# Three output projections by seven products of sums: a change to an attention and gated feed-forward kernel on one core

## The chip, the cores and the metric

The kernel runs on one core of a Trainium2 chip. The core has engines with queues of their own: TensorE (PE; its weight loads are listed as PEld), VectorE (DVE), ScalarE (ACT), GpSimd (POOL) and SyncE (SP), which issues nearly all transfers. TensorE multiplies a stationary tile of up to 128x128 with a moving tile of up to 512 columns and adds the result into PSUM; the other engines work on PSUM (not GpSimd) and on SBUF. The metric is the device time of one execution in microseconds, as the median of the runs.

## The reference

```python
scores = scale * q_c @ k_c^T          # 8 batches x 8 heads, in chunks of 64 positions
attn = softmax(scores); out = attn @ v_c
x = out as [4608 tokens, 512]
g = x @ w_gate;  val = x @ w_val      # [512, 1536] each
y = (g * sigmoid(g) * val) @ w_out    # [1536, 512]
```

Everything is float32. The attention is local to chunks of 64 and small; the three large products make the work.

## The kernel before

Float32 products are made from pairs of a rounded upper part and a rest (`split`: ScalarE casts the upper part, VectorE subtracts it from the whole). Each product is the sum of three matmuls: rest x upper, upper x rest, upper x upper.

The 4608 tokens are nine blocks of 512 (`N`); d_ff is twelve steps `f` of 128. Blocks 0 and 1 and block 2 come first. Blocks 3 to 8 are three pairs, loop `for b in range(3, NB, 2)`, L1306. For a pair, `both_steps` (L1193) runs the twelve gated steps for both blocks together. `gated_pair` (L1152) makes gate and value of two blocks by seven products of sums in place of eight products: the x of the pair is held as seven quarter-size sums `pair.x[0..6]`, the weights as `factors` loaded two steps ahead (L1149), and `seventh` (L878) runs six matmuls of 512 columns for each of the seven. The products go into three PSUM banks, and since products 2, 4 and 6 are added onto product 0 in its bank (`ps1`), ScalarE has to copy the bank (to `h`, then `v`) or VectorE to add it before the next product may go there. SiLU and a multiplication give the step's `h` for the first block and `h2` for the second.

The output projection of the first block stands between these products: `turns` (L889) runs `project` (L537) for the step before, 12 matmuls of 512 columns (4 row tiles of 128 tokens, 3 each, L552 to L554) into four PSUM banks `ps_o`. The `h2` of the second block is kept, and `second_steps` (L1211) runs its twelve projections behind the gated steps, 144 matmuls, while VectorE and ScalarE prepare the next pair's x (`later`). Attention for the next pair (scores, softmax, 32x32 transposes on VectorE, columns) stands in the gated steps as well: `bursts`, `middle`, `behind`.

The orders of TensorE, ScalarE and VectorE are those in which the code is written; those of GpSimd and of SyncE's transfers are set by a scheduler that plans a timeline. Transfers issued by SyncE wait in one queue, so one that has to wait holds up those behind it. Tiles come from pools with a fixed number of buffers, and the wait for a free buffer follows from the pool and the tag.

Of the kernel before, what the change touches and what calls it, by code (L numbers as in the profile page):

```python
# [33 lines left out]
def attn_then_gated_ffn(ctx: ExitStack, tc: tile.TileContext, qk, v, wgv, wo, out):  # L34
# [163 lines left out]
    def save_w(f):  # L198
        kept_w[f] = store.tile([P, 2, 4 * Q], F32, name=f"w{f}")
        nc.sync.dma_start(out=kept_w[f], in_=w_both[f].bitcast(F32))  # L200
# [298 lines left out]
    def out_of_two(f, tag):  # L499

        two = const.tile([P, 2, 2, DM], F32R, name="two", tag=tag)
        nc.sync.dma_start(out=two.bitcast(F32), in_=two_o[f // 2])
        return [(two[:, i, 0], two[:, i, 1]) for i in range(2)]

# [30 lines left out]
    before = []  # L535

    def project(parts, wo_f, which=range(T)):  # L537
        (a, f, hh, hl), (woh, wol) = parts, wo_f
        if not hasattr(a, "o"):
            a.o = [ps_o.tile([P, DM], F32, name="ps_o") for _ in range(T)]  # L540
        for t in which:
            ts, o = slice(t * P, (t + 1) * P), a.o[t]
            final = a.b * N + (t + 1) * P == NT
            ends = final and f == a.steps[1]
            left, right = slice(0, DM // 2), slice(DM // 2, DM)
            parts_of = [(o, slice(0, DM), f == a.steps[0])]
            if ends:
                more = ps_a.tile([P, DM // 2], F32, name="ps_a", tag="ps_a")
                parts_of = [(o[:, left], left, False), (more, right, True)]
            for to, m, first in parts_of:  # L550
                skip = ends and not first
                nc.tensor.matmul(to, hl[:, ts], woh[:, m], start=first, stop=False, skip_group_check=skip)  # L552
                nc.tensor.matmul(to, hh[:, ts], wol[:, m], start=False, stop=False, skip_group_check=skip)  # L553
                nc.tensor.matmul(to, hh[:, ts], woh[:, m], start=False, stop=f in (a.steps[1], a.steps[1] - final), skip_group_check=skip)  # L554
            if final and f == a.steps[1] - 1:
                before.append(ld.tile([P, DM // 2], F32, name="before", tag="qk_t"))
                nc.scalar.activation(before[0], o[:, right], AF.Copy, scale=2.0 ** -8)
            if f == a.steps[1]:

                pools = (hp, "o_sb"), (ld, "v_t")  # L560
                r = a.b * N + t * P

                last = a.b == NB - 1
                halves = 2 if last and t in (0, T - 1) else 1
                for i in range(halves):
                    m = slice(i * DM // halves, (i + 1) * DM // halves)
                    pool, tag = (hp, "hl" if t else "h") if i else pools[t % 2]
                    o_sb = pool.tile([P, DM // halves], F32, name="o_sb", tag=tag)
                    if i and final:
                        nc.vector.scalar_tensor_tensor(out=o_sb, in0=more, scalar=2.0 ** -8, in1=before[0], op0=ALU.mult, op1=ALU.add)  # L570
                    elif i or last and t == T - 2:
                        nc.vector.tensor_scalar_mul(o_sb, o[:, m], 2.0 ** -8)
                    else:
                        nc.scalar.activation(o_sb, o[:, m], AF.Copy, scale=2.0 ** -8)
                    (nc.scalar if final and not i else nc.sync).dma_start(out=out[r:r + P, m], in_=o_sb)
# [568 lines left out]
    def load_weights(f):  # L1144
        tags = (7, 8) if f % 2 == 0 else (9, 10)
        loaded[f] = []
        for kept, tag in zip((kept_w, kept_t), tags):
# [4 lines left out]
    def gated_pair(pair, f, h2, inside, middle):  # L1152
# [23 lines left out]
        if not ending:  # L1176
            turn_of(1)
# [179 lines left out]
```

## Time and profile before

| | us |
|---|---|
| median of 3 runs (lowest, highest) | 891.94 (891.91, 892.08) |
| profiled execution, its own time | 893.19 |
| its span, first to last instruction | 891.4 |
| busy in the span: TensorE | 880.9 |
| weight loads | 729.6 |
| VectorE | 547.2 |
| ScalarE | 388.8 |
| GpSimd | 39.7 |
| transfers: 223.25 MB, mean rate | 250 GB/s |

A row of a group reads: line, engine, operation, written tile <- read tiles, shape, count | busy us, mean ns of one | idle time ahead of the group and what ended it. A row of the timeline reads: start, duration, engine, line, operation. Matmul durations overlap, so TensorE's pace is read from the distance of the starts.

### The profile page before, as it was taken

The numbers are of one execution on the slowest core, as the hardware profiler recorded it, in microseconds if no ns is written. First come the engines' busy times: TensorE is split into PE (matmuls) and PEld (weight loads), VectorE is DVE, ScalarE is ACT, GpSimd is POOL, SyncE is SP. The second block draws the span as 40 slices with busy tenths as digits, with TensorE's granted clock in tenths as the row PEclk, the third lists the DMA queues.
The fourth block names the chain that finished last, engine by engine and source line by source line (L and its number), as shares of the span: only waits on it lengthen the run. The fifth ranks groups of instructions, "written<-read, shape, count | busy, mean of one in ns | idle before, by whom it ended". The sixth has DMA issues, their size and how long they took to land.

```text
span 891.4 us, 14743 instructions
## 1 busy us (share of the span) xinstructions
PE 880.9 (99%) x6034; PEld 729.6 (82%) x6034; DVE 547.2 (61%) x831; ACT 388.8 (44%) x594; POOL 39.7 (4%) x32
## 2 busy tenths in 40 slices
PE   7999999999999999999999999999999999999998
PEld 6788888888888888888888888888888888888886
DVE  5888999673888656776753656767655533333332
ACT  5757777543433345225325444244325432223232
POOL 1100000000055110000000000000000000000000
PEclk9999999999999999999999999999999999999999
DMA  9677778889798777657577757575657575556651
GB/s 358 249 269 279 275 276 320 330 296 350 226 387 276 276 264 242 237 219 255 204 250 291 299 206 270 193 253 225 203 212 281 177 269 202 198 196 232 236 189 47
DMA packets 73314, 223.25 MB, mean 250 GB/s; under 512 B 30752, under 2 KB 31264, under 8 KB 59040
## 3 DMA queue, kind: packets, MB, share of 16 engines
q1 hardware_dynamic: 71664, 219.57, 67.7%
q10 hardware_dynamic: 1584, 2.75, 0.9%
q8 instruction: 47, 0.77, 0.3%
q14 instruction: 19, 0.16, 0.0%
HBM read 178.78 MB, written 43.52 MB: 249 GB/s over the span
## 4 chain that ended last, share of the span: by engine, by line
PE 97%; DMA 1%; DVE 1%; ACT 0%; SPq 0%; issue 0%
PE ps_a L883 27%; PE ps_gv L883 20%; PE ps_gv L478 12%; PE ps_o L552 11%; PE ps_o L554 11%; PE ps_o L553 11%; PE ps_a L290 2%; PE ps_a L368 1%; DMA v_t<-in_v 1%; PE ps_a L468 1%; PE pt L454 0%; PE ps_a L454 0%; DVE z L698 0%; SPq L262 0%; ACT v_t L411 0%; DVE xl L642 0%
## 5 line engine op out<-in xcount | busy, mean ns | idle before, releaser
L883 PE MATMUL ps_a<-x,factors 128*128 128x512 f32 x864 | 219.3, 389 | 0.0
L883 PEld LDWEIGHTS ps_a<-x,factors 128*128 128x128 f32 x864 | 162.2, 188 | 33.7
L883 PE MATMUL ps_gv<-x,factors 128*128 128x512 f32 x648 | 164.4, 389 | 0.0
L883 PEld LDWEIGHTS ps_gv<-x,factors 128*128 128x128 f32 x648 | 121.6, 188 | 25.2
L552 PE MATMUL ps_o<-both,hl 128*128 128x512 f32 x336 | 131.9, 392 | 0.0
L554 PE MATMUL ps_o<-both,hh 128*128 128x512 f32 x336 | 130.7, 389 | 0.0
L553 PE MATMUL ps_o<-both,hh 128*128 128x512 f32 x336 | 130.7, 389 | 0.0
L63 DVE TENSOR_TENSOR hl<-h,hh 128x512 fp32r<-128x512 f32 x98 | 68.2, 696 | 65.5 <-ACT hh L62 65.3
L62 ACT CAST hh<-h 128x512 fp32r<-128x512 f32 x98 | 60.6, 618 | 95.4 <-PE ps_o L554 51.3
L478 PE MATMUL ps_gv<-xh,w 128*128 128x512 f32 x320 | 97.9, 391 | 0.2 <-ACT xh L638 0.2
L887 DVE TENSOR_TENSOR h<-h,ps_gv 128x512 f32<-128x512 f32 x44 | 30.2, 686 | 103.9 <-PE ps_gv L883 103.7
L355 DVE STREAM_TRANSPOSE turned<-s_sb 32x256 f32<-32x256 f32 x192 | 83.7, 436 | 2.7
L522 DVE SCALAR_TENSOR_TENSOR h<-v,h 128x512 f32<-128x512 f32 x88 | 60.8, 691 | 37.7 <-ACT h L1188 33.0
L552 PEld LDWEIGHTS ps_o<-both,hl 128*128 128x128 f32 x336 | 63.1, 188 | 13.5
L554 PEld LDWEIGHTS ps_o<-both,hh 128*128 128x128 f32 x336 | 63.1, 188 | 13.1
L553 PEld LDWEIGHTS ps_o<-both,hh 128*128 128x128 f32 x336 | 63.1, 188 | 12.8
L1188 ACT ACTIVATE h<-ps_a 128x512 f32<-128x512 f32 x36 | 21.5, 598 | 112.1 <-PE ps_a L883 112.1
L478 PEld LDWEIGHTS ps_gv<-xh,w 128*128 128x128 f32 x320 | 59.8, 188 | 12.9 <-ACT xh L638 0.5
L478 PE MATMUL ps_gv<-xl,w 128*128 128x512 f32 x160 | 61.3, 392 | 0.0
L887 DVE TENSOR_TENSOR v<-v,ps_a 128x512 f32<-128x512 f32 x44 | 30.2, 687 | 41.1 <-PE ps_a L883 36.4
L1174 ACT ACTIVATE h<-h 128x512 f32<-128x512 f32 x36 | 22.8, 632 | 52.9 <-DVE h L887 52.9
L887 DVE TENSOR_TENSOR v<-v,ps_gv 128x512 f32<-128x512 f32 x44 | 30.2, 686 | 24.5 <-PE ps_gv L883 24.5
(143 smaller groups left out, 1069.9 us busy)
## 6 DMA issues: line engine op xcount, KB each, us to landing
factors<-w SPq DMA_DIRECT2D x36, 1024.0 KB, 4.8
factors<-t SPq DMA_DIRECT2D x36, 1024.0 KB, 6.1
both<-o SPq DMA_DIRECT2D x70, 512.0 KB, 6.3
w<-w SPq DMA_DIRECT2D x16, 1024.0 KB, 8.1
t<-th SPq DMA_DIRECT2D x24, 512.0 KB, 4.2
two<-o SPq DMA_DIRECT2D x12, 1024.0 KB, 5.2
raw<-in_wgv SPq DMA_DIRECT2D x11, 1024.0 KB, 9.0
qk_t<-in_qk SPq DMA_DIRECT2D x10, 1024.0 KB, 8.1
```

Of the source, the lines that this page charges most:

```text
L62: nc.scalar.copy(out=hi, in_=src)
L63: (engine or nc.vector).tensor_tensor(out=lo, in0=src, in1=hi.bitcast(F32), op=ALU.subtract)
L355: nc.vector.transpose(out=self.turned[to:to + 32, p:p + 2, j, :, 32 * (i % 2):32 * (i % 2) + 32], in_=src[32 * i:32 * i + 32, :, o // 2, 3 ...
L478: nc.tensor.matmul(ps, w, x, start=first and (k, i) == which[0], stop=last and (k, i) == which[-1])
L522: nc.vector.scalar_tensor_tensor(out=h, in0=pv, scalar=2.0 ** -8, in1=h, op0=ALU.mult, op1=ALU.mult)
L552: nc.tensor.matmul(to, hl[:, ts], woh[:, m], start=first, stop=False, skip_group_check=skip)
L553: nc.tensor.matmul(to, hh[:, ts], wol[:, m], start=False, stop=False, skip_group_check=skip)
L554: nc.tensor.matmul(to, hh[:, ts], woh[:, m], start=False, stop=f in (a.steps[1], a.steps[1] - final), skip_group_check=skip)
L883: nc.tensor.matmul(ps, w[u][:, k], x[i][v][:, k], start=first and k == 0 and n == 0, stop=k == NK // 2 - 1 and n == 2, skip_group_check=True)
L887: nc.vector.tensor_tensor(out=t, in0=t, in1=ps, op=ALU.add)
L1174: nc.scalar.activation(h, h, AF.Silu, scale=2.0 ** -8)
L1188: nc.scalar.activation(h2, ps1, AF.Silu, scale=2.0 ** -8)
```

## The change

For each pair, the output projection [1024, 1536] x [1536, 512] is now made by seven products of sums in place of eight. The rows are halved by block, d_ff by even and odd steps, the columns of the output into left and right (`HM`, 256). With A11, A12 the first block's h of even and odd steps, A21, A22 the second's, and B the weights likewise, the seven are A11 B11, A12 B21, and five with S1 = A21 + A22, S2 = S1 - A11, S3 = A11 - A21, S4 = A12 - S2 and sums of the four B.

- In the gated steps only the first two products remain: `Left.project`, 12 matmuls of 256 columns for the step before. They stand in one piece between products 5 and 6, no longer parted over the step (one of four row tiles there and three behind product 6 in steps with attention's products).
- `h` and `h2` stay in `rows`; VectorE makes S3 and S1 of them in steps 3, 4, 8, 9 and 10.
- `second_steps` is replaced by `seven_products`: fifteen units of 24 matmuls of 256 columns. Ahead of each, casts and subtractions split the halves of a later unit (three ahead); banks are copied out (`snapshot`, ScalarE) and added at the end (`finish`, VectorE). The next pair's x is prepared here too.
- The sums of the output weights are made once, in the gated steps of the first pair: GpSimd adds upper and rest of a pair of weight tiles and makes four sums (`out_sums`), ScalarE casts them a step later, GpSimd subtracts (`split_sums`), and four transfers keep them in HBM for all pairs.
- The gated weights' quarter that no product reads is neither kept nor loaded (`save_w`, `load_factors`).
- The transposes of attention are dealt singly: one part ahead of `left.lower`, two at the end of a step.

The order changes on TensorE, ScalarE and VectorE. TensorE before, one gated step of the first pair (`ps_o` is the projection; each group of three is one row tile):

```order
L883 MATMUL ps_a<-x,factors 128x512 x6
L883 MATMUL ps_gv<-x,factors 128x512 x6
L552 MATMUL ps_o<-both,hl 128x512
L553 MATMUL ps_o<-both,hh 128x512
L554 MATMUL ps_o<-both,hh 128x512
```

TensorE of the change, the end of one step and the start of the next:

```order
L1199 MATMUL ps_o<-left,hl 128x256
L1199 MATMUL ps_o<-left,hh 128x256 x2
L858 MATMUL ps_a<-x,factors 128x512 x12
L858 MATMUL ps_gv<-x,factors 128x512 x6
L858 MATMUL ps_a<-x,factors 128x512 x6
```

Product 6 of one step and product 0 of the next follow each other (x12), and nothing stands between product 1 (`ps_gv`) and product 2 (`ps_a`), which adds onto product 0.

ScalarE of the change, from the end of a step of the first pair through the next one (`rows<-ps_a` by L1326 is the SiLU of h2, by L1305 the copy of product 0, `sums<-sums` the cast of GpSimd's sums):

```order
L1326 ACTIVATE rows<-ps_a 128x512
L1169 CAST sums<-sums 128x1024
L1305 COPY rows<-ps_a 128x512
L1307 COPY v<-ps_gv 128x512
L1309 COPY v<-ps_a 128x512
L1313 ACTIVATE rows<-rows 128x512
L1182 CAST hh<-rows 128x512
```

The L1169 cast is new and stands ahead of the copy; before, a step was copy, copy, copy, SiLU, SiLU and the cast of `hh`, with nothing else in most steps.

VectorE of the change, the start of `seven_products` of the first pair (`two` is S2, `halves` the rests of the split parts):

```order
L517 SCALAR_TENSOR_TENSOR rows<-v,rows 128x512
L1216 TENSOR_TENSOR rows<-rows 128x1024
L1216 TENSOR_TENSOR two<-rows 128x1024
L1242 TENSOR_TENSOR halves<-rows,halves 128x1024
L1216 TENSOR_TENSOR two<-rows 128x1024
L1242 TENSOR_TENSOR halves<-two,halves 128x1024
L1216 TENSOR_TENSOR rows<-rows,two 128x1024
```

Where VectorE had only the rests of h2 and the next pair's x behind the gated steps, it now makes sums and rests for every unit.

```diff
+            nc.tensor.matmul(o, hl[:, ts], woh, start=f == a.steps[0], stop=False)
+            nc.tensor.matmul(o, hh[:, ts], wol, start=False, stop=False)
+            nc.tensor.matmul(o, hh[:, ts], woh, start=False, stop=f == a.steps[1])
...
+    def load_factors(f, i):
+        t = const.tile([P, 2, 4 * Q], F32R, name="factors", tag=moved(7 + 2 * (f % 2) + i))
+        for at in (slice(0, 4 * Q),) if i else (slice(0, 2 * Q), slice(3 * Q, 4 * Q)):
+            nc.sync.dma_start(out=t[:, :, at].bitcast(F32), in_=(kept_t if i else kept_w)[f][:, :, at])
+        loaded.setdefault(f, []).append((t[:, 0], t[:, 1]))
...
+    def out_sums(j, engine=nc.gpsimd):
+        t, sums = wide[2].bitcast(F32), wide[3].bitcast(F32)
+        for i in range(2):
+            w = wide[i].bitcast(F32).rearrange("p j (c m) -> p j c m", c=2)
+            engine.tensor_tensor(out=t[:, i::2], in0=w[:, 0], in1=w[:, 1], op=ALU.add)
+        engine.tensor_tensor(out=sums[:, 0:2], in0=t[:, 2:4], in1=t[:, 0:3:2], op=ALU.subtract)
+        engine.tensor_tensor(out=sums[:, 2], in0=t[:, 3], in1=sums[:, 0], op=ALU.subtract)
+        engine.tensor_tensor(out=sums[:, 3], in0=t[:, 1], in1=sums[:, 2], op=ALU.subtract)
...
+            if i - 1 in steps:
+                split_sums(steps.index(i - 1))
+            if i in steps:
+                j = steps.index(i)
+                out_sums(j)
+                if j + 1 < NF // 2:
+                    load_wide(j + 1)
...
+    def split_sums(j, engine=nc.gpsimd):
+        t, sums = wide[2].bitcast(F32), wide[3].bitcast(F32)
+        nc.scalar.copy(out=wide[2], in_=sums)
+        engine.tensor_tensor(out=wide[3], in0=sums, in1=t, op=ALU.subtract)
...
+    class Left:
+        def __init__(self, pair, f, h, w):
+            self.pair, self.f, self.w, self.h = pair, f, w, h
+            self.hh = hp.tile([P, N], F32R, name="hh")
+            self.hl = hp.tile([P, N], F32R, name="hl")
+            nc.scalar.copy(out=self.hh, in_=h)
+        def lower(self):
+            nc.vector.tensor_tensor(out=self.hl, in0=self.h, in1=self.hh.bitcast(F32), op=ALU.subtract)
+        def project(self, which):
+            c = self.pair
+            if not c.banks:
+                for i in (1, 0):
+                    c.banks[i] = [ps_o.tile([P, 2, HM], F32, name="ps_o") for _ in range(2)]
+            for t in which:
+                eighth(c.banks[self.f % 2][t // 2][:, t % 2], self.hh, self.hl, self.w, t,
+                       self.f < 2 and t % 2 == 0)
+    def eighth(to, hi, lo, w, t, first, last=True):
+        ts = slice(t * P, (t + 1) * P)
+        for n, (a, i) in enumerate(((lo, 0), (hi, 1), (hi, 0))):
+            nc.tensor.matmul(to, a[:, ts], w[:, i], start=first and n == 0, stop=last and n == 2, skip_group_check=True)
...
+        def s3(self, j):
+            self.combine(self.rows[0, 0, j], self.rows[0, 0, j], self.rows[1, 0, j], ALU.subtract)
+        def s1_of(self, j):
+            self.combine(self.rows[1, 0, j], self.rows[1, 0, j], self.rows[1, 1, j], ALU.add)
...
+            to = self.rows[2, 0, j] = self.two[:, j % 2]
+            self.combine(to, self.rows[1, 1, j], self.rows[0, 0, j], ALU.subtract)
+        def s4_of(self, j):
+            self.combine(self.rows[0, 1, j], self.rows[0, 1, j], self.rows[2, 0, j], ALU.subtract)
...
+            src = self.rows[((1, 0), (2, 0), (0, 1), (0, 0), (1, 1))[k // 3] + (k % 3,)]
...
+        def unit(self, ps, k, first=False, tiles=range(T)):
+            hi, lo, _ = self.parts[k]
+            for j in range(2):
+                u = 2 * k + j
+                for t in tiles:
+                    eighth(ps(t), hi[:, j], lo[:, j], self.w[u // 4][:, u % 4], t, first and j == 0 and (t % 2 == 0 or t == tiles[0]))
...
+            seventh(ps1, pair.x, loaded[f], 0, True)
+            nc.scalar.copy(out=h, in_=ps1)
+            seventh(ps2, pair.x, loaded[f], 1, True)
+            nc.scalar.copy(out=v2, in_=ps2)
+            seventh(ps1, pair.x, loaded[f], 2, False)
+            nc.scalar.copy(out=v1, in_=ps1)
+            middle.get(f, nothing)()
+            seventh(ps3, pair.x, loaded[f], 3, True)
+            add(h, ps3)
+            nc.scalar.activation(h, h, AF.Silu, scale=2.0 ** -8)
+            seventh(ps1, pair.x, loaded[f], 4, False)
+            add(v2, ps1)
+            seventh(ps2, pair.x, loaded[f], 5, False)
+            add(v1, ps2)
+            times(h, v1)
+            left = Left(pair, f, h, w)
+            mid.get(f, nothing)()
+            left.lower()
+            turns([0] if f in bursts else range(T))
+            if f == NF - 1:
+                pair.s2_of(0)
+            seventh(ps1, pair.x, loaded[f], 6, False)
+            nc.scalar.activation(h2, ps1, AF.Silu, scale=2.0 ** -8)
+            times(h2, v2)
             if f in bursts:
                 turns([1])
                 bursts[f]()
                 turns([2, 3])
...
+        def before_unit(k):
+            if k == 0:
+                pair.s1_of(2)
+                U(2), pair.s2_of(1), L(2), U(3), pair.s2_of(2), L(3)
+            elif k == 1:
+                U(4), pair.s4_of(0), L(4)
+            elif k == 2:
+                U(5), pair.s4_of(1), L(5)
+                each(snapshot, c11, ps1)
+            elif k == 3:
+                U(6), pair.s4_of(2), L(6)
+                each(finish(0, 0), c11, ps3)
+            elif k == 4:
+                each(snapshot, c22, ps2)
+                U(7), XU(0), call("s1"), L(7), XL(0)
+            elif k == 5:
+                U(8), XU(1), call("s4"), L(8), XL(1)
+            elif k == 6:
+                each(snapshot, c12, ps1)
+                U(9), call("s2"), L(9), XU(2)
+            elif k == 7:
+                U(10), XL(2), L(10)
+            elif k == 8:
+                XU(6), U(11), XL(6), L(11)
+            elif k == 9:
+                U(12)
+                each(finish(0, 1), c12, ps2)
+                L(12)
+            elif k == 10:
+                U(13), L(13)
+            elif k == 11:
+                U(14), XU(3), L(14), XL(3)
+            elif k == 12:
+                each(snapshot, c21, ps1)
+                XU(4)
+                each(finish(1, 1), c22, ps1)
+                call("s5"), XL(4)
+            if k in (2, 4, 6, 8):
+                pair.load_sums(3 + k // 2)
+            if n and k in (10, 12, 14):
+                load_factors(*divmod(k // 2 - 5, 2))
...
+        banks = ps2, ps1, ps2, ps1
+        for k in range(3 * 4):
+            before_unit(k)
+            pair.unit(lambda t: banks[k // 3][t // 2][:, t % 2], k, k == 0)
+            if k == 1:
+                turns(range(T))
+        if n:
+            ps6 = [ps_o.tile([P, 2, HM], F32, name="ps_o") for _ in range(2)]
+            for k in range(12, 15):
+                before_unit(k)
+                pair.unit(lambda t: ps6[t // 2][:, t % 2], k, k == 12)
```

More of the change, by code (lines that the diff above doesn't have):

```diff
@@ L497, in out_again @@
         return both[:, 0], both[:, 1]
[L499 to L503, printed above, removed]
     def product(a, f, g):
@@ L542, in project @@
             ts, o = slice(t * P, (t + 1) * P), a.o[t]
[L543 to L557, printed above, removed]
+            nc.tensor.matmul(o, hl[:, ts], woh, start=f == a.steps[0], stop=False)
+            nc.tensor.matmul(o, hh[:, ts], wol, start=False, stop=False)
+            nc.tensor.matmul(o, hh[:, ts], woh, start=False, stop=f == a.steps[1])
             if f == a.steps[1]:
@@ L561, in project @@
                 r = a.b * N + t * P
[L563 to L575, printed above, removed]
+                pool, tag = pools[t % 2]
+                o_sb = pool.tile([P, DM], F32, name="o_sb", tag=tag)
+                nc.scalar.activation(o_sb, o, AF.Copy, scale=2.0 ** -8)
+                nc.sync.dma_start(out=out[r:r + P, :], in_=o_sb)
     pending = []
@@ new lines, in attn_then_gated_ffn, with load_wide @@
+    HM = DM // 2
+    kept_s = store.tile([P, 5 * (NF // 2), 2, HM], F32, name="s")
+    wide = []
+    def load_wide(j):
+        if not wide:
+            wide.extend(wp.tile([P, 2, DM], F32R, name="both", tag="wo") for _ in range(2))
+            wide.append(wp.tile([P, 4, HM], F32R, name="sums", tag="wo"))
+            wide.append(const.tile([P, 4, HM], F32R, name="sums", tag="wo0"))
+        for i in range(2):
+            nc.sync.dma_start(out=wide[i].bitcast(F32), in_=kept_o[2 * j + i])
@@ L1205, in both_steps @@
             behind.get(f, nothing)()
-            pending.append((p, wo_f))
+            for at, what, j in ((3, pair.s3, 0), (4, pair.s1_of, 0), (8, pair.s3, 1), (9, pair.s1_of, 1), (10, pair.s3, 2)):
+                if f == at:
+                    what(j)
+            pending.append((left, None))
             if f + 2 < NF:
                 load_weights(f + 2)
-        pair.kept = kept
-    def second_steps(pair, behind, nothing=lambda: None):
-        def prepare(f):
-            return parts(pair.a[1], f, pair.kept[f // 2][:, f % 2])
-        wo_f = []
-        for f in (0, 2, 4, 6):
-            wo_f += out_of_two(f, moved(7 + f // 2))
-        wo_f += out_again(8), out_again(9)
-        put = [prepare(0)]
-        for f in range(NF):
-            lag(put.pop(0), wo_f[f])
-            if f == 0:
-                wo_f += out_again(10), out_again(11, const, "wo0")
-            if f + 1 < NF:
-                put.append(prepare(f + 1))
-            behind.get(f, nothing)()
-            if not pair.last and f in (4, 8):
-                load_weights(f // 8)
+            elif f == NF - 2:
+                pair.load_sums(0)
+                pair.load_sums(1)
+                pair.upper(0)
+                pair.upper(1)
+                pair.lower(0)
+                pair.lower(1)
+            else:
+                pair.load_sums(2)
+                pair.load_sums(3)
@@ L1327 @@
+        if b == 3:
+            for i in range(8):
+                behind[i] = sums_behind(i, behind.get(i, lambda: None))
+        gated_steps(pair, middle, mid, behind, bursts)
+        seven_products(pair, n)
+        pair = n
 def kernel(**inputs):
```

209 lines of the change are left out of this document (138 added, 71 removed).

## The prediction, written before the result was known

> **What bounds the kernel now.** I read the busy line and the chain of the page first, then the waits of TensorE, then the stretch of one pair.
>
> ```profile
> PE 880.9 (99%) x6034; PEld 729.6 (82%) x6034; DVE 547.2 (61%) x831; ACT 388.8 (44%) x594; POOL 39.7 (4%) x32
> PEclk9999999999999999999999999999999999999999
> PE 97%; DMA 1%; DVE 1%; ACT 0%; SPq 0%; issue 0%
> PE ps_a L290 <- DMA qk_t<-in_qk: 2.7, 2, 1.4
> 327.54:516.30 188.76, 188.76 (x1305) 156.43 (x1304) 120.02 (x185) 77.05 (x118) 0.00 (x0) 1.00 0.69 249
> ```
>
> TensorE is the path: 97% of the chain, full clock. Its longest wait in all is 2.7 us for the first loads, at the start. In the first pair (327.54 to 516.3 us; columns: length, then busy time of PE, PEld, DVE, ACT, POOL, clock, DMA share, GB/s) it is never idle, while VectorE works 120 of 189 us and GpSimd not at all. So the change pays what TensorE sheds, less every wait it puts in.
>
> **TensorE's work.** Before, the output projection of three pairs is 3 pairs x 2 blocks x 12 steps x 4 row tiles x 3 products = 864 matmuls of 512 columns, the last three cut into six of 256. After, it is 7 products x 6 steps x 4 x 3 = 504 matmuls of 256 columns in each pair, 1512 in all. Everything else TensorE does keeps its count. The price of 256 columns is in the last matmuls of the timeline (start, duration, engine):
>
> ```profile
> 885.17 0.39 PE L554 MATMUL ps_o<-both,hh 128*128 128x512 f32 x1
> 886.53 0.39 PE L554 MATMUL ps_o<-both,hh 128*128 128x512 f32 x1
> 886.76 0.28 PE L552 MATMUL ps_o<-both,hl 128*128 128x256 f32 x1
> 886.88 0.28 PE L553 MATMUL ps_o<-both,hh 128*128 128x256 f32 x1
> 886.99 0.28 PE L554 MATMUL ps_o<-both,hh 128*128 128x256 f32 x1
> 887.11 0.28 PE L552 MATMUL ps_a<-both,hl 128*128 128x256 f32 x1
> 887.12 0.19 PEld L553 LDWEIGHTS ps_a<-both,hh 128*128 128x128 f32 x1
> 887.23 0.28 PE L553 MATMUL ps_a<-both,hh 128*128 128x256 f32 x1
> 887.24 0.19 PEld L554 LDWEIGHTS ps_a<-both,hh 128*128 128x128 f32 x1
> 887.35 0.28 PE L554 MATMUL ps_a<-both,hh 128*128 128x256 f32 x1
> ```
>
> Durations overlap; starts count. From 885.17 to 886.53 there are six gaps: 0.227 us for 512 columns. Among the six narrow ones the gaps are 0.12, 0.11, 0.12, 0.12, 0.12. I take 0.12, since the last three, with loads and matmuls in an even beat, show it; the mean of the five is 0.118. Half of 0.227 is 0.1135, so a narrow matmul loses 0.0065 of its gain. Before: 861 x 0.2267 + 6 x 0.118 = 195.9 us. After: 1512 x 0.12 = 181.4. The term is **-14.5 us** (-17.5 at 0.118). One eighth of the multiplications, 24.5 us of 195.9, is left out, and 10 of it go back to the shorter shape. The upper bound is a load's 0.19 of duration per matmul, if loads did not overlap: 1512 x 0.19 = 287, a rival below.
>
> The Trainium skill, in "TensorE: Matmul & The Clock Gate", section "Back-to-back issue gap", gives N/2.4 + 2.5 ns when warm, so 109 ns for 256 columns and 216 for 512. The sum by it would be 165 against 186, so -21; the rows (0.12 and 0.227) disagree, and the measurement decides.
>
> **The gated steps.** A step falls from 42 x 0.2267 + 12 x 0.2267 = 12.24 to 42 x 0.2267 + 12 x 0.12 = 10.96 us, and the projection no longer parts products 1 and 2. Product 2 adds onto the bank that the copy `h` (now L1305) reads, so copy, 0.59, must fit into product 1's 1.36. It does where ScalarE is free. VectorE's step is six operations of 0.69, 4.1 us; with a third of a block's transposes (12 x 0.45 = 5.4) and one combination (1.25) it is 10.7 in steps 3 and 8, just inside 10.96. The places where ScalarE is not free follow.
>
> ```profile
> L371 ACT COPY s_sb<-ps_a 128x512 f32<-128x512 f32 x24 | 12.3, 600 | 4.8 <-PE ps_a L368 4.8
> L62 ACT CAST x<-s_sb 128x1024 fp32r<-128x1024 f32 x18 | 18.7, 1047 | 3.7 <-DVE s_sb L1120 3.1 <-DMA t<-th 0.5
> L1165 ACT COPY h<-ps_a 128x512 f32<-128x512 f32 x36 | 21.2, 588 | 42.1 <-PE ps_a L883 42.1
> 669.01 2.09 PE ps_a L368 x126
> L522 DVE SCALAR_TENSOR_TENSOR h<-v,h 128x512 f32<-128x512 f32 x88 | 60.8, 691 | 37.7 <-ACT h L1188 33.0 <-ACT h L1174 1.1
> L355 DVE STREAM_TRANSPOSE turned<-s_sb 32x256 f32<-32x256 f32 x192 | 83.7, 436 | 2.7
> ```
>
> At the end of step 10 in pairs one and two, attention's last products (2.09 us of TensorE), four copies of 0.60 out of them and two casts of 1.05 stand ahead of step 11's copy: 0.36 + 1.05 + 4 x 0.6 + 2 x 1.05 + 0.59 = 6.5 us after product 6 (with handoffs 6.8), and product 2 is due at 0.36 + 2.09 + 0.72 + 2 x 1.36 = 5.9. Two waits of 0.9: **+1.7 us**; 0 if the copies start earlier, 3 if late.
>
> **The sums of the output weights (pair one only).** This is where TensorE can lose most. Six times GpSimd makes four sums of a pair of weight tiles, ScalarE casts them at a step's end (L1169), right ahead of the next copy `h`, GpSimd subtracts, and four stores take them away.
>
> ```profile
> 285.44 2.39 POOL L165 TENSOR_TENSOR th<-th 128x1024 fp32r<-128x1024 f32 x1 [1.04 <-ACT th L162]
> 287.79 1.30 POOL L148 TENSOR_TENSOR th<-th 128x512 f32<-128x512 f32 x1
> 289.16 0.74 POOL L149 TENSOR_TENSOR th<-th 128x256 f32<-128x256 f32 x1
> 319.31 2.40 POOL L165 TENSOR_TENSOR th<-th 128x1024 fp32r<-128x1024 f32 x1 [22.27 <-ACT th L162]
> 320.22 2.58 DVE L63 TENSOR_TENSOR x<-s_sb,x 128x1024 fp32r<-128x1024 f32 x1 [1.21 <-ACT x L62]
> 306.51 1.23 DVE L63 TENSOR_TENSOR x<-sum,x 128x1024 fp32r<-128x1024 f32 x1 [1.12 <-ACT x L62]
> 269.58 2.94 DVE L327 TENSOR_TENSOR s_sb<-s_sb,z 128x2048 f32<-128x2048 f32 x1
> 270.45 2.67 POOL L149 TENSOR_TENSOR th<-th 128x256 f32<-128x256 f32 x1
> 358.62 2.29 DVE L327 TENSOR_TENSOR s_sb<-s_sb,z 128x2048 f32<-128x2048 f32 x1
> DMA to landing us min/median/max: 2.0/8.1/8.7
> t<-th SPq DMA_DIRECT2D x24, 512.0 KB, 4.2
> ```
>
> From one cast to the copy behind the next: cast 1.05; the upper half's store has to land (L) before GpSimd may write that tile, meanwhile the subtract, 2.40; two additions and a difference of 512 elements, 3 x 1.30; two of 256, 2 x 0.74; cast 1.05; copy 0.59. With some 0.4 of handoffs (0.07 each: 1.12 idle around a 1.05 cast) that is 8.5 + max(L, 2.5). Available are 10.96 + 2.72 - 0.8 = 12.9 us, from 0.8 after one product 6 to the next step's product 2. Two engines also get in each other's way: at 320.22 VectorE's operation on two tiles of SBUF takes 2.58 instead of 1.23, and ends 1.1 after GpSimd's does; at 270.45 GpSimd takes 2.67 instead of 0.74. A step has three such VectorE operations of 0.69; I let two of them delay the chain, 1.4.
>
> L was 2.0 us in the quiet and 8.1 behind other loads for the 256 KB stores of the output (that row is for the o_sb tiles of pair one's gated steps), and 4.2 for the 512 KB stores beside loads of 1024 KB, as here; I take 4.2. There are four intervals with sums on both ends (casts at the ends of steps 1-2, 2-3, 5-6, 6-7; the others have an idle step or the start ahead). In two of them the chain is 12.7 + 1.4, 1.2 too long. In the other two the softmax's multiply (2.29, on two tiles of SBUF) starts just as the subtract ends: sums then start at 6.75 instead of 6.1 after product 6 and collide with all three operations; added up, the copy ends 2.5 late. Sum 2 x 1.2 + 2 x 2.5 = **+7.4 us**. With L at 2.0 only the two with the multiply are left, some 3; with L at 8.1 it is 2 x 5.1 + 2 x 5.7 = 21.6.
>
> **The five products behind the steps.** Per pair 360 matmuls and the last 12 of the steps, 44.6 us, in 15 units of 24 (2.88 us). VectorE has 30 operations of 1024 elements and eight of 512 there.
>
> ```profile
> 310.76 1.22 DVE L1116 TENSOR_TENSOR s_sb<-s_sb 128x1024 f32<-128x1024 f32 x1
> 312.01 1.22 DVE L1120 TENSOR_TENSOR s_sb<-sum,s_sb 128x1024 f32<-128x1024 f32 x1
> L1188 ACT ACTIVATE h<-ps_a 128x512 f32<-128x512 f32 x36 | 21.5, 598 | 112.1 <-PE ps_a L883 112.1
> ```
>
> Starts 1.25 apart: 30 x 1.25 + 8 x 0.69 = 43 us, as long as the products. The first halves made here are used in unit 2, at 2 x 2.88 + 1.44 = 7.2 us; they need SiLU 0.6, the product 0.69, a sum 1.25, a cast 1.05 and a subtract 1.25 with handoffs, 5.4. The tightest is unit 9, at 27.4: up to its own subtract VectorE has 19 operations of 1.25 and two of 0.69, behind the 1.5 of the last step's, so 26.6, and 26.8 with handoffs. The margin is half a microsecond, so I put **+0.5 us** for all pairs, 0 to 6. Pair three has no next x to prepare and is free. The removed second steps had no wait to give back, and the end (last matmul, a 256-column VectorE operation, a 128 KB store) has the same parts as before: 0.
>
> **Sum.** -14.5 + 1.7 + 7.4 + 0.5 = -4.9 us. The profiled execution has a span of 891.4 and took 893.19; the median of the runs is 891.94, so I take the change off the median: **887.0 us**.
>
> **Rivals.** *The sums are hidden* (stores land in 2 to 3 us, VectorE and GpSimd seldom meet): -14.5 + 2.2 + 0 to 3, so 879.6 to 883. For it: the 2.0 of a quiet store. Against: the collisions above do not depend on stores.
>
> *GpSimd's chain sets the step* (the other side). With L the price is 2 (L - 3.0) + 5 + 2 (L - 4.9 if positive); it eats the 12.3 us that are left at L = 5.8, and is slower than before by over 0.2% from L = 6.3. At 8.1 the time is 891.94 - 12.3 + 21.6 = 901. For it: 8.1 is the median of pair one's own 256 KB stores, and a step with sums moves 768 + 1024 KB of factors, 256 of left weights, 1024 of weights for the sums and 1024 of sums, 4.19 MB in 10.96 us, 383 GB/s.
>
> ```profile
> 480.00:516.30 36.30, 36.30 (x279) 30.26 (x279) 22.30 (x25) 19.12 (x29) 0.00 (x0) 1.00 0.83 311
> ```
>
> 311 GB/s at a DMA share of 0.83 makes some 375 at full share, 11.2 us a step: by itself 0.2 x 6, but queues would be full and L long. Against: the 8.1 came behind 2 MB of queries and factors asked for at once. The Trainium skill, "DMA: Bandwidth & Descriptors", "Specifications", puts HBM at about 358 GB/s for a core; by that a step would take 11.7 us. The row's 375 is what I go by.
>
> *Weight loads do not keep up* in a long row: 1512 x 0.19, so 891.94 + 91 = 983. Against: loads at 887.12 and 887.24 are 0.12 apart.
>
> *The products starve on VectorE*: 3 us a pair, 891.94 - 4.9 + 9 = 896.
>
> **Chances.** Forecast (chain costs 4 to 12): 0.57, 883.5 to 891.5, at 887.0. Hidden: 0.22. GpSimd's chain: 0.16. Loads: 0.01. Starving: 0.04. A measurement of this kernel tells about 0.2%, 1.8 us, from no change, so faster means under 890.2: 0.22 and nine tenths of 0.57, 0.73. Same: a tenth of the forecast, a third of GpSimd's chain, 0.11. Slower: 0.16. Eight in ten: 879.5 to 896.
>
> **What would show it.** Right: narrow matmuls 0.12 apart in the products, no wait ahead of units; TensorE's waits list copy `h` (rows<-ps_a, L1305), in pair one at steps 3, 4, 7 and 8 with about 1 to 2.5 us each behind the L1169 cast, and at step 11 under 1 us; VectorE operations on SBUF alone lengthened while POOL is busy. Wrong: TensorE without waits in pair one (hidden), waits of 4 us and more there with the GpSimd additions waiting for a DMA (its chain), a gap above 0.13 between narrow matmuls (loads), or waits on `halves` (starving).

## The result and the profile after

The changed kernel takes 903.24 us, the median of 6 runs (901.21 to 905.68). The kernel before takes 891.97 beside it (891.76 to 892.08). The ratio is 1.0127 (95% interval 1.0108 to 1.0147): 11.3 us slower, where 887.0 had been predicted, with a range up to 896. The profiled execution is one of the faster of the six, with 901.28 us and a span of 899.5, 8.1 more than before.

The busy line, the clock row and the chain of the page after:

```profile
PE 874.9 (97%) x6679; PEld 753.0 (84%) x6679; DVE 638.6 (71%) x898; ACT 418.6 (47%) x609; POOL 91.2 (10%) x68
PEclk9999999999999999899999999999999999999999
PE 85%; DMA 5%; ACT 3%; issue 3%; DVE 2%; POOL 2%; SPq 0%; DVEq 0%; POOLq 0%
```

TensorE is busy for 6.0 us less than before and still the kernel is slower: the chain now leaves TensorE for 15% of the span, and the clock row has an 8 where there was none. The waits of TensorE (engine, tile and line, what it waited for: us in all, times, longest):

```profile
PE ps_a L858 <- ACT rows L1305: 10.8, 4, 5.4
PE ps_a L291 <- ACT rows L1326: 2.4, 4, 1.2
PE ps_a L369 <- ACT rows L1326: 1.8, 4, 0.4
```

The first is the forecast wait for the copy behind the cast, at 10.8 us. The other two are attention's products, which wait for the SiLU that reads product 6; no step of the prediction had them. Three stretches (length, busy time of PE, PEld, DVE, ACT, POOL, clock, DMA share, GB/s), pair one, pair two, and the 372 narrow matmuls behind pair one's steps:

```profile
327.30:532.45 205.15, 193.06 (x1534) 168.52 (x1533) 153.57 (x206) 91.19 (x130) 50.34 (x36) 0.98 0.79 259
532.45:720.56 188.11, 185.60 (x1523) 163.54 (x1521) 145.36 (x207) 84.03 (x120) 0.00 (x0) 1.00 0.62 202
487.98:532.40 44.42, 44.42 (x372) 44.42 (x372) 39.38 (x39) 23.83 (x28) 0.00 (x0) 1.00 0.86 275
```

Pair one went from 188.8 to 205.15, pair two from 188.8 to 188.11, pair three (its last matmul starts 175.5 us after its first) by 6.7 down, and the start and the end gave 0.8: together the 8.1. The loss is in pair one alone. One interval there, from the timeline of all engines (start, duration, engine, line, operation; in brackets the idle time ahead and what ended it):

```profile
355.35 2.42 POOL L1170 TENSOR_TENSOR sums<-sums 128x1024 fp32r<-128x1024 f32 x1 [6.47 <-ACT sums L1169]
364.80 2.97 POOL L1146 TENSOR_TENSOR sums<-both 128x512 f32<-128x512 f32 x2 [7.04 <-issue]
370.32 0.72 POOL L1149 TENSOR_TENSOR sums<-sums 128x256 f32<-128x256 f32 x1
371.07 1.04 ACT L1169 CAST sums<-sums 128x1024 fp32r<-128x1024 f32 x1 [5.90 <-POOL sums L1149]
372.02 0.58 ACT L1305 COPY rows<-ps_a 128x512 f32<-128x512 f32 x1
372.14 0.37 SPq L1173 DMA_DIRECT2D s<-sums  x1
372.66 2.93 PE L858 MATMUL ps_a<-x,factors 128*128 128x512 f32 x6 [5.40 <-ACT rows L1305]
375.38 2.76 PE L858 MATMUL ps_gv<-x,factors 128*128 128x512 f32 x6
379.36 1.52 PE L858 MATMUL ps_gv<-x,factors 128*128 128x512 f32 x6
379.88 2.54 POOL L1146 TENSOR_TENSOR sums<-both 128x512 f32<-128x512 f32 x2 [5.32 <-DMA s<-sums]
```

Read it from the top. GpSimd's subtract ends at 357.8 and its next additions start at 364.80, 7 us later. In the next round they start 7.7 after the store of 372.14 and the profile names that store. The cast waits 5.90 for GpSimd, the copy for the cast, and TensorE 5.40 for the copy. Then six matmuls take 2.93 and 2.76 us, where six take 1.52 at full clock.

### The profile page after: what moved, and what is told of

It reads as the page before. It is cut to its first block, busy times and chain, and to the rows that moved or that the text cites. A ratio compares the mean times of both kernels' runs of the same rounds, so it can differ in the third digit from the quotient of the medians.

```text
span 899.5 us, 16294 instructions
## 1 busy us (share of the span) xinstructions
PE 874.9 (97%) x6679; PEld 753.0 (84%) x6679; DVE 638.6 (71%) x898; ACT 418.6 (47%) x609; POOL 91.2 (10%) x68
## 4 chain that ended last, share of the span: by engine, by line
PE 85%; DMA 5%; ACT 3%; issue 3%; DVE 2%; POOL 2%; SPq 0%; DVEq 0%; POOLq 0%
PE ps_a L858 23%; PE ps_gv L858 18%; PE ps_o L1199 13%; PE ps_gv L479 11%; PE ps_gv L1199 6%; PE ps_o L539 3%; PE ps_o L540 3%; PE ps_o L541 3%; PE ps_a L291 1%; PE ps_a L369 1%; DMA out<-o_sb 1%; DMA raw<-in_wgv 1%; DMA qk_t<-in_qk 1%; POOL sums L1146 1%; DVE rows L517 1%
## 5 line engine op out<-in xcount | busy, mean ns | idle before, releaser
L858 PE MATMUL ps_a<-x,factors 128*128 128x512 f32 x864 | 219.4, 394 | 10.8 <-ACT rows L1305 10.8
L858 PEld LDWEIGHTS ps_a<-x,factors 128*128 128x128 f32 x864 | 160.3, 190 | 44.6 <-ACT rows L1305 13.2
L1199 PE MATMUL ps_o<-sums,halves 128*128 128x256 f32 x630 | 76.6, 283 | 0.0
L1199 PEld LDWEIGHTS ps_o<-sums,halves 128*128 128x128 f32 x630 | 76.0, 192 | 0.0
L862 DVE TENSOR_TENSOR rows<-rows,ps_gv 128x512 f32<-128x512 f32 x36 | 24.7, 686 | 71.8 <-PE ps_gv L858 65.7
L517 DVE SCALAR_TENSOR_TENSOR rows<-v,rows 128x512 f32<-128x512 f32 x72 | 54.0, 750 | 12.6 <-ACT rows L1326 5.5
L539 PE MATMUL ps_o<-both,hl 128*128 128x512 f32 x144 | 56.5, 392 | 0.0
L540 PE MATMUL ps_o<-both,hh 128*128 128x512 f32 x144 | 56.1, 390 | 0.0
L541 PE MATMUL ps_o<-both,hh 128*128 128x512 f32 x144 | 56.1, 389 | 0.0
L1199 PE MATMUL ps_o<-left,hh 128*128 128x256 f32 x288 | 53.8, 283 | 0.0
L1199 PE MATMUL ps_gv<-sums,halves 128*128 128x256 f32 x432 | 53.3, 283 | 0.0
L1199 PEld LDWEIGHTS ps_gv<-sums,halves 128*128 128x128 f32 x432 | 52.7, 192 | 0.2
L1242 DVE TENSOR_TENSOR halves<-rows,halves 128x1024 fp32r<-128x1024 f32 x36 | 43.3, 1222 | 11.2 <-ACT halves L1238 11.2
L1238 ACT CAST halves<-rows 128x1024 fp32r<-128x1024 f32 x36 | 37.0, 1051 | 28.1 <-PE ps_gv L1199 9.2
```

What stands on the lines that cost most here:

```text
L517: nc.vector.scalar_tensor_tensor(out=h, in0=pv, scalar=2.0 ** -8, in1=h, op0=ALU.mult, op1=ALU.mult)
L539: nc.tensor.matmul(o, hl[:, ts], woh, start=f == a.steps[0], stop=False)
L540: nc.tensor.matmul(o, hh[:, ts], wol, start=False, stop=False)
L541: nc.tensor.matmul(o, hh[:, ts], woh, start=False, stop=f == a.steps[1])
L858: nc.tensor.matmul(ps, w[u][:, k], x[i][v][:, k], start=first and k == 0 and n == 0, stop=k == NK // 2 - 1 and n == 2, skip_group_check=True)
L862: nc.vector.tensor_tensor(out=t, in0=t, in1=ps, op=ALU.add)
```

## The experiments

**The price of the chain, and which of its links is long.** The first kernel leaves the sums out and fills their places with stores of the same size; the second makes the sums but stores something else, so that nothing waits for a store to land.

```diff
-        t, sums = wide[2].bitcast(F32), wide[3].bitcast(F32)
-        nc.scalar.copy(out=wide[2], in_=sums)
-        engine.tensor_tensor(out=wide[3], in0=sums, in1=t, op=ALU.subtract)
...
-            nc.sync.dma_start(out=of_j[:, 0:2, h], in_=src[:, 0:3:2])
-            nc.sync.dma_start(out=of_j[:, 3:5, h], in_=src[:, 1:4:2])
+            for i in range(2):
+                nc.sync.dma_start(out=of_j[:, 3 * i:3 * i + 2, h], in_=kept_o[2 * j + h][:, :, i * HM:(i + 1) * HM])
```

> Left out: the loads, additions, casts and subtractions of the output weights' sums; their places in memory are filled with unsummed weights by stores of the same size, at the same steps, so the output is not the reference's. Theory (the sums' chain in pair one holds TensorE: 10.4 us of waits and some 5 of slow clock behind them): 903.2 - 16 = 887, steps 3, 4 and 8 back at 10.98 and 13.95. Rival (the extra traffic or the narrow products cost it): above 897, with waits of TensorE on other tiles in pair one.

Measured: 888.71 us, ratio to before 0.9966 (0.9952 to 0.9979).

> Changed: the stores keep size, number and place, but take unsummed weights from memory in place of the sums, so additions need not wait for a store to land (the output is not the reference's). GpSimd's work, casts and collisions stay. Theory (landing of 7 us sets the chain): chain 8.5 + 2.5 + 1.4 = 12.4 against 12.9 available, waits of TensorE behind the cast under 2 us in all, no slow clock, 886 to 890. Rival (GpSimd's and VectorE's collisions, or late loads, set it): waits of 6 us and more stay, 897 to 903.

Only the last three lines of the diff are in this one. Measured: 890.14, ratio 0.9982 (0.9973 to 0.9991). Pair one of the first and of the second kernel (the clock of 0.95 in the first row is not in the times: its steps take the same 10.98 us as elsewhere):

```profile
329.56:519.22 189.66, 188.03 (x1534) 165.85 (x1532) 145.63 (x206) 85.95 (x124) 0.00 (x0) 0.95 0.68 216
```

```profile
330.86:521.74 190.88, 188.63 (x1533) 165.71 (x1532) 150.00 (x206) 91.33 (x130) 55.03 (x36) 1.00 0.75 246
```

Against 205.15, the whole of the sums cost 15.5 us in the profiled execution. With GpSimd's work, casts, collisions and amount of traffic kept and only the wait for the landing taken out, 14.3 of it is gone. So the landing of the stores is what made the chain too long; the rest of the sums (GpSimd's own pace, VectorE, the loads of the weights) cost 1.2. (The whole times carry 2.3 and 3.6 us of a later start of pair one, 329.56 and 330.86 in place of 327.30, so pair one is what to compare.)

**Why the landing takes so long.** Three kernels: the stores of the upper halves issued by ScalarE in place of SP; the sums laid out so that a store moves pieces of 4 KB in place of 1 KB; and the loads of the weights for sets two to six left out.

```diff
-            nc.sync.dma_start(out=of_j[:, 0:2, h], in_=src[:, 0:3:2])
+            (nc.sync, nc.scalar)[h == 0].dma_start(out=of_j[:, 0:2, h], in_=src[:, 0:3:2])
```

> The two stores of the sums' upper halves are issued by ScalarE, right behind its cast, and not by SP behind the loads. If their place in SP's queue makes them late: landing falls from some 7 us to 4, the waits of pair one from 10.4 to 3 or less, 889 to 894. If full DMA engines make them late: landing stays 6 to 8 us, 900 to 905, a little worse by ScalarE's issuing time ahead of the copy.

```diff
-    kept_s = store.tile([P, 5 * (NF // 2), 2, HM], F32, name="s")
+    kept_s = store.tile([P, NF // 2, 2, 4, HM], F32, name="s")
...
-            nc.sync.dma_start(out=of_j[:, 0:2, h], in_=src[:, 0:3:2])
-            nc.sync.dma_start(out=of_j[:, 3:5, h], in_=src[:, 1:4:2])
+            nc.sync.dma_start(out=kept_s[:, j, h], in_=src)
```

> The sums lie in memory so that each set's halves are stored in one piece of 4 KB for a partition, and not in four of 1 KB, and two stores take the place of four; loads behind the steps then read in pieces of 2 KB, one for each sum. If small packets make the stores late: landing falls from 6.5 to 4 us, waits from 10.4 to 3 or less, 890 to 895. If the volume ahead in the DMA engines does: landing stays over 6 us, 900 to 905.

```diff
                 out_sums(j)
-                if j + 1 < NF // 2:
-                    load_wide(j + 1)
```

> Left out: the loads of the output weights for sets two to six, 5 MB of the traffic of pair one's first steps; the sums are made six times from the first two weight tiles, so the output is not the reference's. GpSimd's work, casts, the waits for the stores and the stores themselves stay. If the stores land late because the DMA engines are full with what lies ahead: landing falls from 6.5 to about 4 us, and by the price of the prediction, 2 (L - 3.0) + 5, the waits from 10.4 to 3 to 7 with no or one slow stretch: 890 to 895. If a store of this kind takes 6 to 8 us by itself: 900 to 904.

Measured: 909.13 (ratio 1.0197, 1.0183 to 1.0210), 907.66 (1.0174, 1.0160 to 1.0188) and 895.96 (1.0044, 1.0029 to 1.0060). The stores of the sums between 340 and 446 us (queue, count, KB each, median us from issue to landing) of the changed kernel, then of the three in this order:

```profile
s<-sums SPq DMA_DIRECT2D x24, 256.0 KB, 6.5
```

```profile
s<-sums ACTq DMA_DIRECT2D x12, 256.0 KB, 7.5
s<-sums SPq DMA_DIRECT2D x10, 256.0 KB, 6.4
```

```profile
s<-sums SPq DMA_DIRECT2D x11, 512.0 KB, 6.3
```

```profile
s<-sums SPq DMA_DIRECT2D x24, 256.0 KB, 4.2
```

Another queue lands in 7.5 us and longer pieces in 6.3, so neither the place in SP's queue nor the size of the pieces makes it. Less volume does: 4.2 as the median, and pair one takes 199.58 us, 5.6 less. The changed kernel's step that begins with the first cast, and the same step with the loads left out:

```profile
353.40:364.40 11.00, 11.00 (x56) 9.35 (x55) 10.19 (x13) 4.78 (x8) 2.42 (x1) 1.00 1.03 355
```

```profile
354.30:365.30 11.00, 11.00 (x56) 9.34 (x55) 10.17 (x13) 4.77 (x8) 2.39 (x1) 1.00 0.87 265
```

A DMA share of 1.03 at 355 GB/s: the DMA engines had hardly a free moment in that step. The Trainium skill, "DMA: Bandwidth & Descriptors", section "Issuing engines are not separate DMA queues", says that transfers started by different engines run on the same 16 DMA engines and interleave; the 7.5 us on ScalarE's queue agree.

But the share of a step is not the whole answer, for with the loads left out the first set's stores landed no sooner. GpSimd's next additions still wait 7.89 us for them, and TensorE's longest wait, in step 3, is 6.0 us where it was 5.4:

```profile
366.52 3.06 POOL L1146 TENSOR_TENSOR sums<-both 128x512 f32<-128x512 f32 x2 [7.89 <-DMA s<-sums]
PE ps_a L858 <- ACT rows L1303: 7.9, 3, 6.0
```

What that kernel saves, it saves almost all in steps 4 and 8. The rows of SP say more than the median. In the changed kernel a store that is issued close behind the step's largest load, 1024 KB of factors, lands late, and one issued well behind it lands soon:

```profile
355.96 0.41 SPq L1126 DMA_DIRECT2D factors<-t  x1
357.37 0.36 SPq L1173 DMA_DIRECT2D s<-sums  x1
```

```profile
432.31 0.34 SPq L1126 DMA_DIRECT2D factors<-t  x1
438.22 0.36 SPq L1173 DMA_DIRECT2D s<-sums  x1
```

The first of these two stores landed after 7.3 us, the second after 2.1. Over the six sets the first store was issued 1.4, 2.0, 3.2, 5.6, 2.0 and 5.9 us behind that load and landed after 7.3, 7.6, 6.2, 3.9, 7.6 and 2.1. So 6.5 is a median of very different landings, and the long ones stand right behind loads asked for at once. This is read from the rows; no kernel here moves the stores away from the factors and changes nothing else.

Why the two changes of form made it worse is only half known. With ScalarE issuing, it is ScalarE itself that was held up, with the copy behind it:

```profile
360.42 0.38 ACTq L1173 DMA_DIRECT2D s<-sums  x1
361.37 0.58 ACT L1305 COPY rows<-ps_a 128x512 f32<-128x512 f32 x1 [5.25 <-DMA v_t<-in_v]
```

Its cast had ended at 356.1 and its transfer was issued at 360.42; the profile names a load of v, and what ties the two together was not tried. With the long pieces the first two intervals from one subtract of GpSimd to the next are 19.9 and 16.2 us, for 16.9 and 15.1 in the changed kernel, and the waits behind the cast 14.3 us in all; what lengthened them stays open.

**Ways round it.** If landing is the long link, buffers for two more sets should free the chain from it, and casts that stand where nothing waits should free TensorE from the chain.

```diff
+        sums_of[j] = [ld.tile([P, 4, HM], F32R, name="sums", tag="qk_t") for _ in range(2)] if j in (1, 4) else wide[2:]
+        t, sums = (u.bitcast(F32) for u in sums_of[j])
```

> The second and the fifth set of sums get tiles of their own (two of the attention loads' tiles, free at that time), so the additions of sets one to five seldom wait for the stores of the set before; casts, stores and order stay, and the output is whole. Theory (landing of 7 us sets the chain): chain about 1.05 + 2.4 + 5.9 + 0.4 = 9.8 from cast to cast, under a step's 10.98; the waits behind the cast fall from 10.4 to 0 to 2, no slow clock: 886 to 890. Rival (loads of the weights, late by the same full DMA engines, take the place): waits of 4 and more stay, 894 to 900.

Measured: 900.13, ratio 1.0092 (1.0079 to 1.0105). The time is the rival's. TensorE's waits, and rows of GpSimd and SP:

```profile
PE ps_a L858 <- ACT rows L1309: 4.7, 2, 4.3
PE ps_gv L858 <- DMA factors<-t: 4.0, 2, 2.9
PE ps_a L858 <- DVE v L862: 1.9, 1, 1.9
```

```profile
356.55 1.26 POOL L1149 TENSOR_TENSOR sums<-both 128x512 f32<-128x512 f32 x1 [8.99 <-DMA both<-o]
357.77 0.72 POOL L1152 TENSOR_TENSOR sums<-sums 128x256 f32<-128x256 f32 x1
357.84 4.29 SPq L1139 DMA_DIRECT2D both<-o  x2
362.22 1.22 SPq L1126 DMA_DIRECT2D factors<-w  x2
```

Two orders, both made by the scheduler, took the place of the landing. On GpSimd an addition of the second set stands ahead of the last operation of the first (L1152) and waits for its weights until 356.55, so the first cast is late. In SP's queue the next set's weights, which wait for GpSimd to free their tiles, stand ahead of the next step's factors, so these are late: 4.0 us.

```diff
-            for i in range(8):
-                behind[i] = sums_behind(i, behind.get(i, lambda: None))
+            behind[0] = sums_behind(0, behind.get(0, lambda: None))
+            for j, (to, i) in enumerate(((middle, 2), (middle, 3), (middle, 4), (middle, 6), (middle, 7), (middle, 8))):
+                to[i] = split_at(j, to.get(i, lambda: None))
```

> Only the six casts of the sums (and what follows them) move from the ends of steps 1-3 and 5-7 to the middle of steps 2-4 and 6-8, behind the copy v1, where no product waits for ScalarE for some 4 us more; stores and the waits for them stay. If the chain of 15 us from cast to cast sets the pace whatever stands behind the cast: three sets in three steps still come some 5 us late in each group of three, 896 to 900. If only the copy behind the cast mattered: 886 to 890.

Measured: 893.77, ratio 1.0022 (1.0013 to 1.0031), between the two numbers. The waits behind the copy:

```profile
PE ps_a L858 <- ACT rows L1308: 3.1, 3, 1.7
```

The chain is not much shorter (casts at 359.17 and 373.08, 13.9 apart), but 3.1 us of waits replace 10.8, and none is followed by a slow clock. Casts that come some 4 us later, with the subtractions, stores, additions and loads that follow them, gave 9.5 of the 11.3 us back. The stores also land sooner here, after 5.5 us as the median in place of 6.5, so the share of the cast's place alone is not told apart.

**Attention's products.** Their wait for the SiLU that reads product 6 was first taken for a lack of TensorE work between the two.

```diff
-            turns([0] if f in bursts else range(T))
+            if f not in bursts:
+                turns(range(T))
...
-                turns([1])
+                turns([0, 1])
```

> At the four steps with attention products, turn 0 goes behind product 6, next to turn 1, so 0.72 us of TensorE and not 0.36 stand between product 6 and attention's first products. Theory (these wait for SiLU's reading of product 6, 4.2 us in eight places, since the turns became half as long): 2.5 to 4 us less, 899.5 to 901. Rival (the wait only moves behind, to the next step's copy): within 1 us of 903.2.

Measured: 903.55, ratio 1.0133 (1.0112 to 1.0154), no change, and the steps stay at 13.95. The theory fell. A step with attention's products in pair two of the changed kernel shows what it missed:

```profile
598.43 1.55 PE L858 MATMUL ps_a<-x,factors 128*128 128x512 f32 x6
599.86 0.62 ACT L1182 CAST hh<-rows 128x512 fp32r<-128x512 f32 x1 [2.88 <-DVE rows L517]
600.38 0.59 ACT L1326 ACTIVATE rows<-ps_a 128x512 f32<-128x512 f32 x1
601.03 2.09 PE L291 MATMUL ps_a<-qk_t 64*64 64x64 f32 x126 [0.45 <-ACT rows L1326]
```

Product 6 ends before 600, but ScalarE first makes the cast `hh`, which waits for VectorE's two operations behind product 5. The SiLU comes behind it wherever the turns stand. The next kernel puts product 6 and its SiLU first:

```diff
+            if f in bursts:
+                left = Left(pair, f, h, w)
+                mid.get(f, nothing)()
+                left.lower()
             times(h2, v2)
             if f in bursts:
-                turns([1])
+                turns([0, 1])
```

> At the four steps with attention products, product 6 and its SiLU go ahead of the cast hh on ScalarE, and turns 0 and 1 behind product 6. The run with the turns alone moved left each such step at 13.95: theory now (the SiLU stands behind hh, which waits for two VectorE operations after product 5, so it ends 2.9 us after product 5 however the turns lie): each step with attention products falls from 13.95 to 13.3 in pairs one and two, 0.65 x 6 and 0.5 in the first, 4.4 less: 898 to 900. Rival (the cast hh and what hangs on it come late instead): steps stay at 13.9.

Measured: 899.48, ratio 1.0080 (1.0062 to 1.0099). The same step:

```profile
599.75 0.60 ACT L1327 ACTIVATE rows<-ps_a 128x512 f32<-128x512 f32 x1 [2.66 <-PE ps_a L858]
600.24 0.61 ACT L1182 CAST hh<-rows 128x512 fp32r<-128x512 f32 x1
600.35 2.14 PE L291 MATMUL ps_a<-qk_t 64*64 64x64 f32 x128
```

No wait, and the step takes 13.20 in place of 13.95. Pair two fell from 188.11 to 185.19, 2.9 us, and pair one's steps 0, 5 and 10 by 0.6, 0.75 and 0.75. With 0.75 for step 8, where the chain's wait covers it, both pairs together make 5.8 us. Of the median 3.8 us went.

**All together.** The two buffers, the SiLU first and the casts of the first three sets in the middle of the steps (the last three at the ends of 5, 6 and 7):

> Tiles of their own for sets two and five, SiLU of product 6 first at the steps with attention products, and the casts of the first three sets moved into the middle of steps 2, 3 and 4, behind the copy v1, the others at the ends of 5, 6 and 7. By the two theories all of pair one's waits but those of the first step go: 903.2 - 16 - 4.4 = 882 to 885, under the kernel before by 0.8%. Rival: late loads or the first stage, which moved by 3 us between runs, leave 886 to 890.

Measured: 886.90, ratio 0.9950 (0.9934 to 0.9967): faster than both kernels, but not the 882 to 885 expected; the time is the rival's. What is left in pair one is mostly SP's order, in the profiled run (889.31 us, 2.4 above the median), at 369.96:

```profile
PE ps_gv L858 <- DMA factors<-t: 3.3, 1, 3.3
```

Two kernels put the loads of the weights behind the next step's factors.

> As the run with all three edits (886.9), but the loads of the output weights stand behind the next step's factors in SP's queue, since there they wait for GpSimd with the factors behind them (3.3 us of TensorE's waits for factors in step 3, with 3.4 us of half clock). If that is the cause: pair one falls from 195.3 by 4 to 5 us, 882 to 884. Rival: the additions now start later and the cast is late instead, 886 to 889.

Here the loads were written behind the additions that use them, so sets three to six are made from the weights of the set before; its time stands for that order of transfers alone. Measured: 886.93, ratio 0.9949 (0.9937 to 0.9962). It has no wait for factors, but 3.7 us of waits for VectorE's additions (L862), and the time has not moved.

```diff
             if f + 2 < NF:
                 load_weights(f + 2)
+                later.get(f, nothing)()
...
+            with tc.issue_after(last_factors[0]):
+                load_wide(j)
```

> The run with all three edits (886.9), whole, and the loads of the output weights for sets three to six issued only behind the factors that the step's end asks for, so that SP does not hold factors back while GpSimd frees the tiles. If the wait for factors in step 3 (3.3 us, and the half clock behind it, 5.3 in that step) is due to that order: pair one under 191.5 (195.3 in the run with three edits), 882 to 885. Rival: the weights come late instead and with them the casts, or VectorE's collisions take the place, 885 to 888.

Measured: 884.95, ratio 0.9926 (0.9913 to 0.9940), the whole computation: 7.0 us under the kernel before and 18.3 under the change. Against the 886.90 with three edits it is 2.0 us, and the two intervals still touch. Pair one and its waits:

```profile
326.43:519.02 192.59, 188.36 (x1534) 165.00 (x1532) 157.77 (x206) 91.40 (x130) 53.99 (x36) 1.00 0.84 281
```

```profile
PE ps_a L858 <- DVE v L862: 3.1, 2, 1.7
PE ps_a L858 <- ACT rows L1321: 0.8, 2, 0.4
PE ps_gv L858 <- DMA factors<-t: 0.7, 1, 0.7
```

The waits behind the copy (L1321) are down to 0.8 us although the stores of the sums still land late, after 7.3 us as the median: with tiles of their own for two sets and three casts in the middle of steps, TensorE hardly waits for them any more. Step 3 fell from 16.24 to 11.27 us, but step 7 rose from 11.52 to 13.33, where VectorE's addition is late. So the order of transfers was the cause of that wait, and 1.8 of the 5.0 us gained went to step 7: pair one is at 192.59, for 195.28, and not under 191.5 as expected.

## Why the prediction was wrong

It added four terms to -4.9 us. The profiled execution says +8.1. Of the 13.0 us between them the sums' chain makes 8.1 and the waits of attention's products 4.1 more than the 1.7 set down for step 11's copy; what remains is small.

- **TensorE's work, -14.5: right.** The 372 narrow matmuls behind pair one's steps take 44.42 us, 0.119 each (0.12 taken), in the long row as in the six from which the price was read. By the same counts pair three should lose 25 x 12 x 0.2267 - 504 x 0.12 = 7.5, and lost 6.7.
- **The five products, +0.5: nothing.** No wait on `halves` stands in the list, and 372 x 0.12 = 44.6 is what they took. Starving on VectorE did not happen.
- **Step 11's copy, +1.7: the wrong place, and too small.** That wait did not come: all but 0.4 us of the 10.8 are in steps 3, 4 and 8 of pair one. In its stead attention's products waited at all eight places, 4.2 us by the list, 5.8 by the run that took it away. The step that failed is the one that looked only at what stands ahead of the copy `h`. The SiLU that reads product 6 now has the cast `hh` in front of it, which stood behind it before, and the run that turned these two round took the wait away. The cover has also shrunk: before, 0.68 us of wide matmuls stood between product 6 and attention's products; after, 0.36. What that part alone cost was not tried.
- **The sums' chain, +7.4: 15.5.** The mechanism was right, link by link: cast, store, additions, cast, copy, in steps 3 and 4 and 8 (in step 7 it cost nothing). The price as a function of the landing L, 2 (L - 3.0) + 5 + 2 (L - 4.9), gives 15.2 at the measured 6.5, but see below; with the median of L back at 4.2, by the kernel with one load, pair one stands at 199.58, 9.9 above the one without sums, against 7.4. The step that failed is the size of L, 4.2 for 6.5, and with it the clock behind a long wait, which the prediction put at nothing. L was read from 512 KB stores beside other loads, as if the load on the DMA engines were alike. The prediction had the number that speaks against it: 4.19 MB a step need 383 GB/s and some 375 were there. It used it for a rival of 0.16 and not for L. It also had a row of 8.1 us for stores behind 2 MB asked for at once, and set it aside; the stores of the sums stand behind such loads in four of the six sets, and the first of each set landed there after 6.2 to 7.6 us.

That the formula met the sum is luck: its four waits are three, of 5.40, 1.31 and 3.73, together 10.4, and of the 5.1 that remain 4.5 are something that it does not contain. After the two long waits the clock is halved. The stretch right behind the first, in the view by stretches:

```profile
372.60:376.00 3.40, 3.34 (x8) 2.68 (x9) 0.00 (x0) 0.87 (x3) 1.96 (x1) 0.50 1.04 296
```

Six matmuls then take 2.93 and 2.76 us behind the first wait, and 2.31 and 2.49 behind the other, for 1.52 each: 1.41 + 1.24 + 0.79 + 0.97 = 4.4, with 0.06 in a fifth group 4.5.

By terms and pairs: pair one -2.1 (narrow matmuls; the 12 wide ones of block 2 are still in it) + 15.5 + 2.9 = +16.3, as measured. Pair two -4.8 + 2.9 and 1.2 that remain, most of it in its steps 0 and 1; step 0 has no projection between its products. This was not taken apart further. The rival *GpSimd's chain sets the step* is what happened, at a median of 6.5 instead of 8.1 us of landing; it was given 0.16. The further 2 us from the profiled run to the median are not taken apart; the run with the turns alone, whose edit does not touch the sums, had 208.6 in pair one, with the waits behind the copy at 13.8, so the chain's waits differ from run to run.

## What to carry to other kernels

Price a transfer on which something waits by what the DMA engines are asked for just ahead of it, not by a like transfer elsewhere: the same 256 KB store landed after 2.1 us well behind the step's loads and after 7.3 us close behind them, and each chain through it grows by the difference. An operation that depends on such a chain belongs where no other work of its engine is due (casts placed 4 us later, with what follows them, gave 9.5 us), and a load that waits for a tile to come free belongs behind those that don't wait. When orders change, look up for every operation that frees a bank what now stands ahead of it, not only for the one that is being priced (turning the cast and the SiLU round gave 5.8 us).

## What the runs showed of the hardware

- **The clock after a wait.** In these kernels each wait of TensorE in the gated steps of 1.91 us and more (1.91, 2.49, 2.68, 3.19, 3.40, 3.73, 5.40, 6.70 among them) was followed by 3.4 or 6.8 us at half clock; those of 1.31, 1.61, 1.68, 1.69 and 1.81 were not. The Trainium skill, "TensorE: Matmul & The Clock Gate", section "Why this matters for your kernels", advises against gaps above about 3 us. Here shorter ones were enough: behind the changed kernel's waits of 5.40 and 3.73 us the slow matmuls cost 2.7 and 1.8 us more.
- **Narrow matmuls keep their pace.** 0.119 to 0.12 us for 256 columns, with a weight load for each, held over 372 in a row.
- **GpSimd and VectorE.** In the 106 us with sums (340 to 446) the mean of VectorE's 512-element operations on two tiles of SBUF (L517, L1185) was 1.00 us, where it was 0.69 in the same stretch before; those that read PSUM stayed at 0.69. The prediction had assumed such a delay. It cost TensorE little: all that the sums cost with the wait for the landing out of the way is 1.2 us.
